# GpSimd's turn on the shared port is taken from the instruction in front of VectorE's last port user, with the port's release as traced and a new policy table

## The chip, the cores and the metric

The kernel runs on one core of one Trainium2 chip. The metric is the device time of one execution in microseconds (us). TensorE is called PE, VectorE DVE, ScalarE ACT, GpSimd POOL and SyncE SP, as in the profile; SP only issues DMAs here.

## The reference

```python
xn = layernorm(x)                                   # x: 1 x 2048 x 512, bf16
q, k, v = heads(xn @ wqkv)                          # 32 heads of 16
p = softmax(q @ k.T * 16 ** -0.5)                   # 2048 x 2048 in each head
A = (p @ v) @ wo
h = layernorm(xn)
u = gelu(einsum("bsd,sf->bdf", h, w1) + b1)         # along the sequence: 2048 -> 1376
B = transpose(einsum("bdf,fs->bds", u, w2) + b2)    # 1376 -> 2048
out = x + A + B
```

The attention takes nearly all of the time: 32 heads of 2048 x 2048 exponentials.

## The kernel before

**Tiles.** The scores are made in 1024 tiles of 128 x 1024: 32 blocks (a block is a quarter of the queries for four heads) times 16 groups of keys times two head pairs. PE writes a tile's scores into two PSUM banks (`L799`, two matmuls a tile; `L789` in the last block). The exponential of a tile is made in one of two ways. Either ACT makes it (name `exp`, `L825`), which gives one bf16 tile; or DVE makes it (name `dexp`, `L834`) by adding a constant and converting to int16, so that the bits read as bf16 are an approximate exponential. Such a tile then needs three more copies of itself with other constants added (`SHIFTS`, name `sh`, `L840`: int16 128 x 1024, SBUF to SBUF). The shifts are shared between DVE and POOL. PE multiplies each of the tiles with V (`L881`, `L870`, four matmuls a tile), so an ACT tile costs PE one such group and a DVE tile four. Where the two banks of a tile lie side by side, `exp` and `dexp` are one instruction of 1024 elements; otherwise they are two of 512.

**Other work.** Projections (`L929`, `L985`), the token mixing's two products (also `L929`), PSUM evictions on DVE (`L955`, `L974`, `L995`, `L1031`, `L1077`, `L1103`), small normalisation steps and the scaling of VM (`L635`, `L688`) and the division by the softmax sum (`L1142`) on POOL. `L726` are matmuls without use that keep PE's clock up where the plan leaves PE idle.

**Order.** A planner in the kernel's own Python (class `Sched` and the `while True` loop) decides, when the program is built, which engine does what and in which order. It has a cost for every operation, keeps the time at which each engine is free, and takes the candidate that can start first. The loop's choices are steered by a policy of eight numbers; `PLAN` is a string of 64 base-36 digits, one for each 16 tiles, that names the policy in `POLICIES`. The planned times are not in the program: it holds each engine's instructions in order, and semaphore waits between them.

**The shared port.** An operation with `port=True` is one that uses the SBUF port which DVE and POOL share: the shifts on both engines and all POOL work. The planner keeps `port_free` for both engines (when the port is free of that engine). `port_time` holds back the start of a port operation accordingly, `_time` sets `port_free`, and `add` makes each POOL operation wait, by a semaphore, for DVE's last port user:

```python
if port and eng == "pool" and self.port_op is not None:
    deps.add(self.port_op)
if port and eng == "dve":
    self.port_op = op
```

DVE never waits for POOL because of the port. In the loop, a POOL shift becomes a candidate only if the time until DVE's next port operation (or until DVE is free) is at least `SH_I` = 1.11 less a slack of the policy.

Of the kernel before, what the change touches and what calls it, by code (L numbers as in the profile page):

```python
# [58 lines left out]
SEM = 0.05  # L59
PE_SWITCH = 0.10  # L60
PE_LAT = 0.38
PV_T = 0.1095
POOL_AFTER = 0.03
AS_I, AS_L = 0.8, 0.9
EXP_I, EXP_L = 0.904, 1.03
EXPH_I, EXPH_L = 0.477, 0.60
# [17 lines left out]
SH_I, SH_L = 1.11, 1.05  # L84
# [12 lines left out]
PLAN_STEP = 16  # L97
PLAN = tuple(int(c, 36) for c in "00f41j96ioe4283j88076r8jjti283fos8rs08tig23g0ih10n7tg0i05608f5v6")
URGENT = ("kv0", "qt", "kt", "vt")
URG_DUE = 24  # L100
UT0, UT_STEP = 196, 31
# [8 lines left out]
class Op:  # L110
# [3 lines left out]
    def __init__(self, eng, fn, name=""):  # L114
        self.eng = eng
        self.fn = fn
        self.pos = -1
        self.deps = []
        self.signals = False
        self.waits = []  # L120
        self.is_dma = False
        self.dma_sem = None
        self.dma_val = 0
        self.q = None
        self.after = None
        self.name = name
        self.t0 = 0.0
        self.t1 = 0.0


class Sched:
    ENGS = ("pe", "act", "dve", "pool", "sp")

    def __init__(self, nc, es):
        self.nc = nc
        self.es = es
        self.streams = {e: [] for e in self.ENGS}
        self.order = []
        self.last_writer = {}
        self.readers = {}  # L140
        self.dma_ops = []
        self.free = {e: 0.0 if e in ("sp", "act") else 0.7 for e in self.ENGS}
        self.busy = {e: 0.0 for e in self.ENGS}
        self.pe_mode = None
        self.pe_end = 0.0
        self.pe_tiles = {}
        self.port_free = {"dve": 0.0, "pool": 0.0}
        self.port_op = None
        self.act_end = 0.0
        self.pe_work = []  # L150
        self.filler = None
        self.pend = []
# [85 lines left out]

    def port_time(self, eng, t):

        return max(t, self.port_free["pool"] if eng == "dve" else self.port_free["dve"] + POOL_AFTER)

    def _time(self, op, cost, ready, port):
        eng = op.eng
        if port:
            ready = self.port_time(eng, max(self.free[eng], ready))
        if op.is_dma:
            op.t0 = max(self.free[eng], ready)
            self.free[eng] = op.t0 + cost[0]
            op.t1 = op.t0 + cost[1]  # L250
        elif eng == "pe":
            mode, tiles, dur = cost
            t = max(self.free["pe"], ready)
            if mode != self.pe_mode:
                t = max(t, self.pe_end + PE_SWITCH)
                self.pe_mode = mode
                self.pe_tiles = {}
            for x in tiles:
                t = max(t, self.pe_tiles.get(x, 0.0))
            for x in tiles:  # L260
                self.pe_tiles[x] = t + dur
            self.pe_end = max(self.pe_end, t + dur)
            self.free["pe"] = t + 0.004
            self.busy["pe"] += dur * len(tiles) / 4.0
            op.t0, op.t1 = t, t + dur + PE_LAT - 0.214
            self.pe_work.append((t, dur, len(tiles) / 4.0))
        else:
            op.t0 = max(self.free[eng], ready)
            self.free[eng] = op.t0 + cost[0]
            self.busy[eng] += cost[0]  # L270
            op.t1 = op.t0 + cost[1]
            if eng == "act":
                op.t1 = max(op.t1, self.act_end + cost[0] + (EXP_GAP if op.name == "exp" else 0.0))
                self.act_end = op.t1
                self.free[eng] = max(self.free[eng], op.t1 - ACT_QUEUE)
        if port:
            self.port_free[eng] = op.t0 + cost[0]

    def add(self, eng, fn, reads=(), writes=(), name="", dma=False, out_dma=False, cost=None, port=None):
        op = Op(eng, fn, name)  # L280
        op.is_dma = dma
        op.q = "o" if out_dma else "i"
        if cost is None:
            cost = (DMA_I, DMA_L) if dma else (("F", (0, 1, 2, 3), 0.22) if eng == "pe" else (EV_I, EV_L))
        deps = self._deps(eng, reads, writes, dma)
        deps.discard(op)
        if port is None:
            port = eng == "pool" and not dma
        ready = self.ready(eng, reads, writes, dma)
        if eng == "pe" and self.filler is not None:  # L290
            self.pend = [k[1] for k in writes if k[0] == "bank"] if name == "sc" and cost[2] > 0.2 else []
            self.keep_clock(ready, cost)
        self._time(op, cost, ready, port)
        if port and eng == "pool" and self.port_op is not None:
            deps.add(self.port_op)
        if port and eng == "dve":
            self.port_op = op
        op.deps = list(deps)
        for k in reads:
            self.readers.setdefault(k, []).append(op)  # L300
        for k in writes:
            self.last_writer[k] = op
            self.readers[k] = []
        op.pos = len(self.streams[eng])
        self.streams[eng].append(op)
        self.order.append(op)
        if dma:
            self.dma_ops.append(op)
        return op
# [79 lines left out]
def bass_parallel_sum__softmax_full_mha__mixer_token_mlp__prompt_kernel(  # L389
# [18 lines left out]
    with ExitStack() as es:  # L408
# [415 lines left out]
        def exp_specs(n):  # L824
            return [dict(eng="act", fn=lambda e, cs=cs, src=src: e.activation(buf(pbuf[n])[:, cs], src, ACTF.Exp, scale=LN2_128),  # L825
                         reads=[("bank", k) for k in ks], writes=half_keys(free_p[0], cs), name="exp",
                         cost=(EXP_I, EXP_L) if side(n) else (EXPH_I, EXPH_L)) for cs, src, ks in parts(n)]
# [5 lines left out]
        def dexp_spec(n, w):  # L833
            return [dict(eng="dve", fn=lambda e, cs=cs, src=src: e.tensor_scalar(  # L834
                buf_i(w)[:, cs], src, IBIAS, 0.0, ALU.add, ALU.max),
                reads=[("bank", k) for k in ks], writes=half_keys(w, cs), name="dexp",
                cost=(P1_I, P1_L) if side(n) else (P1H_I, P1H_L)) for cs, src, ks in parts(n)]
# [491 lines left out]
        def h_ok():  # L1329
            return next_n >= H_AT + H_STEP * h_n[0] and all(("xT", t) in have for t in range(NT))  # L1330
# [45 lines left out]
        def est(specs):  # L1376
            s0 = specs[0]
            r = 0.0
            for s_ in specs:
                r = max(r, sc.ready(s_["eng"], s_["reads"], s_["writes"]))  # L1380
            t = max(sc.free[s0["eng"]], r)
            if s0.get("port"):
                t = sc.port_time(s0["eng"], t)
            return t
# [102 lines left out]
        while True:  # L1487
            if next_n >= plan_at and plan_at < NN:
                d_steal, p_keep, dead_slack, pe_fit, ext_rank, d_back, d_fly, p_slack = POLICIES[PLAN[plan_at // PLAN_STEP]]
                plan_at += PLAN_STEP  # L1490
# [11 lines left out]
            if ready_q and free_p:  # L1502
                el = []
                for n in ready_q:
                    sp_ = exp_specs(n)
# [6 lines left out]
            if ready_q and fly < d_fly and len(free_p) >= 4 + p_keep:  # L1512
                act_free = sc.free["act"]
                for qi, n in enumerate(ready_q):
                    if NN - n <= D_END:
                        continue
                    sp_ = dexp_spec(n, free_p[0])
                    t = est(sp_)
# [6 lines left out]
            for j in sh_jobs:  # L1525
                if j["ok"]():
                    sp_ = shift_spec("dve", j["w"], j["o"], j["k"])
# [11 lines left out]
            pl = []  # L1539
            dve_port = min([z[0] for z in dl if z[2] == "shd" or (z[2] == "gen" and z[3]["cur"][1][0].get("port"))] + [1e9])  # L1540
            for j in sh_jobs:
                if NN - j["n"] <= POOL_END:
                    continue
                sp_ = shift_spec("pool", j["w"], j["o"], j["k"])
                pl.append((est([sp_]), 1, "shp", (j, sp_), SH_I))
            for g in frees + exts:
                if g["cur"] and g["cur"][0] == "pool":
                    pl.append((est(g["cur"][1]), 0, "gen", g, 1.25))
            if hgen is not None and h_ok():
                pl.append((max(sc.free["pool"], next_h), 2, "h", None, 0.67))  # L1550
            pl = [z for z in pl if max(dve_port, sc.free["dve"]) - z[0] >= z[4] - p_slack]
# [6 lines left out]
            sp_, e_s = None, 1e9  # L1558
# [3 lines left out]
            if next_n < NN and pv_grp >= grp(vblk(next_n)) - 1 and len(free_banks) >= 2 + spare and score_has(next_n):  # L1562
                s_ = best_pair()
                banks_of[next_n] = s_
                sp_ = score_specs(next_n)
# [44 lines left out]
            if not cands:  # L1610
                pl = [z for z in ([] if not sh_jobs else [(0, 0, "shd", (sh_jobs[0], shift_spec("dve", sh_jobs[0]["w"], sh_jobs[0]["o"], sh_jobs[0]["k"])))])]
# [12 lines left out]
            elif kind == "exp":  # L1624
                n, sp_ = what
                ready_q.remove(n)
                exp_commit(n)
                for z in sp_:
                    add(z)
                free_banks.extend(banks_of[n])  # L1630
            elif kind == "dexp":
                n, sp_ = what
# [3 lines left out]
                for z in sp_:  # L1636
                    add(z)
# [8 lines left out]
            elif kind in ("shd", "shp"):  # L1646
                j, sp_ = what
# [15 lines left out]
            elif kind == "gen":  # L1663
                g = what
# [9 lines left out]
            elif kind == "score":  # L1674
                n, sp_, s_ = what
# [6 lines left out]
            elif kind == "pv":  # L1682
# [4 lines left out]
                if pv_left[b] == 0:  # L1687
                    g = dict(gen=task_spill() if b < 0 else task_epilogue(b) if b < NBLK - 1 else task_tail(b - NBLK + 1), cur=None)
# [4 lines left out]
            elif kind == "ext":  # L1693
                g = what
# [21 lines left out]
            for i, (rel, due, nm, gen, need) in enumerate(ext_tasks):  # L1716
# [19 lines left out]
                g = dict(gen=gen, cur=None, due=due, name=nm)  # L1736
# [63 lines left out]
```

## Time and profile before

| | |
|---|---|
| median of 3 runs | 698.47 us (698.19 to 698.93) |
| the profiled execution | 698.7 us |
| its span, first to last instruction | 696.8 us, 29995 instructions |
| PE busy | 686.3 us (98%), 13225 matmuls |
| ACT busy | 678.4 us (97%), 789 instructions |
| DVE busy | 663.6 us (95%), 1198 |
| POOL busy | 388.6 us (56%), 436 |
| granted PE clock | 1.000 |

The profiled execution lies 0.23 us above the median, and 1.9 us lie outside its span. Busy time is the union of an engine's instructions in the trace. Successive instructions of ACT and of DVE overlap in the records (the next one begins before the one in front has ended), so the cost of one in a row of them is taken from end to end, not from its recorded duration.

### The profile page before, as it was taken

How to read it: one execution, taken by the hardware profiler on the slowest of the kernel's cores; microseconds unless marked ns; L12 is line 12 of the kernel's file. 1: busy time of each engine (PE TensorE's matmuls, PEld its weight loads, DVE VectorE, ACT ScalarE, POOL GpSimd, SP SyncE). 2: the span in 40 equal slices, each digit the busy share in tenths (PEclk: the TensorE clock that was granted, in tenths of full speed). 3: DMA queues.
4: the chain of work that ended last, by engine and by line, in shares of the span. 5: the costliest groups of instructions: out<-in, count | busy, mean ns of one | idle time of the engine just before them, and what ended most of it. 6: DMA issues, size and time to landing. Idle time of an engine off the chain costs nothing.

```text
span 696.8 us, 29995 instructions
## 1 busy us (share of the span) xinstructions
PE 686.3 (98%) x13225; PEld 317.4 (46%) x13225; DVE 663.6 (95%) x1198; ACT 678.4 (97%) x789; POOL 388.6 (56%) x436
## 2 busy tenths in 40 slices
PE   8999999999999999999999999999999999999998
PEld 6544444444444444444454444444444444444444
DVE  7888979999999999998999999999999999989997
ACT  7999999999999999999999999999999999999996
POOL 6856744356565556555555565555555545545654
PEclk9999999999999999999999999999999999999999
DMA  7410131101122121220222213121220102112111
GB/s 225 66 25 13 45 79 27 30 6 32 43 45 56 40 61 41 49 56 20 43 48 59 63 31 79 45 49 29 47 61 23 48 25 64 46 45 63 38 30 45
DMA packets 88756, 33.86 MB, mean 49 GB/s; under 512 B 70514, under 2 KB 88626, under 8 KB 88626
## 3 DMA queue, kind: packets, MB, share of 16 engines
q1 hardware_dynamic: 87810, 31.56, 19.4%
q8 instruction: 103, 1.69, 1.0%
q10 hardware_dynamic: 816, 0.39, 0.2%
q14 instruction: 27, 0.22, 0.1%
HBM read 21.70 MB, written 2.35 MB: 35 GB/s over the span
## 4 chain that ended last, share of the span: by engine, by line
PE 65%; DVE 22%; ACT 9%; issue 2%; POOL 1%; DMA 1%; DVEq 0%; POOLq 0%
PE ps L881 23%; PE ps L799 23%; PE ps L929 16%; DVE pT L834 8%; ACT pT L825 7%; DVE pT L840 5%; DVE x_sb L834 3%; ACT x_sb L825 2%; DVE x_sb L840 2%; PE ps L985 1%; DVE OT L1103 1%; DMA xnT<-hx 1%; PE ps L870 0%; DVE Qall L955 0%; DVE osb L1077 0%
## 5 line engine op out<-in xcount | busy, mean ns | idle before, releaser
L825 ACT ACTIVATE pT<-ps 128x1024 bf16<-128x1024 f32 (+1 forms) x570 | 528.3, 1105 | 5.3 <-PE ps L799 5.2
L799 PE MATMUL ps<-QT,KT 32*128 32x512 bf16 x1976 | 276.0, 384 | 1.8 <-DVE pT L834 0.4
L834 DVE TENSOR_SCALAR pT<-ps 128x1024 int16<-128x1024 f32 (+1 forms) x265 | 263.6, 1011 | 10.1 <-PE ps L799 9.8
L881 PE MATMUL ps<-pT,V 128*32 128x256 bf16 x4624 | 245.0, 275 | 1.4 <-DVE OT L1103 0.3
L840 POOL TENSOR_SCALAR pT<-pT 128x1024 int16<-128x1024 int16 x158 | 165.1, 1045 | 124.0 <-DVE pT L840 86.5
L825 ACT ACTIVATE x_sb<-ps 128x1024 bf16<-128x1024 f32 (+1 forms) x197 | 201.2, 1089 | 1.2 <-PE ps L799 1.2
L799 PEld LDWEIGHTS ps<-QT,KT 32*128 32x128 bf16 x1976 | 76.7, 91 | 169.9 <-ACT pT L825 72.7
L881 PEld LDWEIGHTS ps<-pT,V 128*32 128x32 bf16 x4624 | 111.4, 96 | 73.8 <-issue 52.7
L840 DVE TENSOR_SCALAR pT<-pT 128x1024 int16<-128x1024 int16 x317 | 127.6, 428 | 0.4
L834 DVE TENSOR_SCALAR x_sb<-ps 128x1024 int16<-128x1024 f32 (+1 forms) x110 | 110.8, 1022 | 2.7 <-PE ps L799 1.8
L881 PE MATMUL ps<-x_sb,V 128*32 128x256 bf16 x1712 | 109.1, 275 | 0.4 <-DVE x_sb L840 0.3
L840 POOL TENSOR_SCALAR pT<-x_sb 128x1024 int16<-128x1024 int16 x64 | 66.9, 1045 | 49.9 <-DVE pT L840 39.0
L840 POOL TENSOR_SCALAR x_sb<-pT 128x1024 int16<-128x1024 int16 x57 | 59.6, 1045 | 38.3 <-DVE pT L840 27.5
L881 PE MATMUL ps<-pT,VM 128*32 128x256 bf16 x912 | 64.7, 275 | 0.9 <-POOL VM L688 0.5
L929 PE MATMUL ps<-hx,wblk 128*32 128x512 bf16 x688 | 59.9, 384 | 0.0
L881 PEld LDWEIGHTS ps<-x_sb,V 128*32 128x32 bf16 x1712 | 43.8, 96 | 25.4 <-issue 19.5
L840 DVE TENSOR_SCALAR pT<-x_sb 128x1024 int16<-128x1024 int16 x133 | 54.3, 429 | 0.2
L840 DVE TENSOR_SCALAR x_sb<-pT 128x1024 int16<-128x1024 int16 x110 | 45.9, 424 | 0.1
L929 PE MATMUL ps<-wkv_raw,wblk 128*32 128x512 bf16 x512 | 44.6, 385 | 0.0
L1142 POOL TENSOR_TENSOR oT<-oC,denb 128x256 bf16<-128x256 f32 (+1 forms) x32 | 23.3, 728 | 29.5 <-DVE pT L840 16.2
L840 POOL TENSOR_SCALAR x_sb<-x_sb 128x1024 int16<-128x1024 int16 x24 | 25.1, 1045 | 18.5 <-DVE pT L840 15.6
L881 PEld LDWEIGHTS ps<-pT,VM 128*32 128x32 bf16 x912 | 24.2, 96 | 15.7 <-issue 9.7
(124 smaller groups left out, 461.4 us busy)
## 6 DMA issues: line engine op xcount, KB each, us to landing
wblk<-in_B_w_dram SPq DMA_DIRECT2D x10, 512.0 KB, 4.6
wblk<-in_B_w_dram SPq DMA_DIRECT2D x16, 320.0 KB, 3.6
oC<-OT SPq DMA_DIRECT2D x248, 16.0 KB, 1.9
denb<-rden_scratch SPq DMA_DIRECT2D x124, 32.0 KB, 1.9
xr<-in_A_x_dram SPq DMA_DIRECT2D x16, 128.0 KB, 2.3
out_dram<-osb SPq DMA_DIRECT2D x16, 128.0 KB, 2.0
QT<-Qall SPq DMA_DIRECT2D x120, 16.0 KB, 1.9
x_sb<-in_A_x_dram SPq DMA_DIRECT2D x2, 512.0 KB
```

The source lines that it names most:

```text
L799: specs.append(dict(eng="pe", fn=lambda e, r=r, bk=bk: e.matmul(bank(bk), lhsT=KT[32 * r:32 * r + 32, T, 128 * kt:128 * (kt + 1)], rhs=QT[ ...
L825: return [dict(eng="act", fn=lambda e, cs=cs, src=src: e.activation(buf(pbuf[n])[:, cs], src, ACTF.Exp, scale=LN2_128), reads=[("bank", k) ...
L834: return [dict(eng="dve", fn=lambda e, cs=cs, src=src: e.tensor_scalar(buf_i(w)[:, cs], src, IBIAS, 0.0, ALU.add, ALU.max), reads=[("bank" ...
L840: return dict(eng=eng, fn=lambda e: e.tensor_scalar(buf_i(o), buf_i(w), float(SHIFTS[k]), 1.0, ALU.add, ALU.mult), reads=[("pT", w), ("pTh ...
L881: specs.append(dict(eng="pe", fn=lambda e, c=c, h=h, i=i, off=off: e.matmul(bank(pv_bank[vb])[32 * c:32 * c + 32, 256 * par:256 * par + 25 ...
L929: specs.append(dict(eng="pe", fn=lambda e, c=c, w=w: e.matmul(bank(ex)[32 * c:32 * c + w, :], lhsT=lhs_of(32 * c, 32 * c + w), rhs=rhs, st ...
L985: specs.append(dict(eng="pe", fn=lambda e, ct=ct, c=c, i=i, t=t: e.matmul(bank(ex)[32 * c:32 * c + 32, 128 * i:128 * (i + 1)], lhsT=xnT[:, ...
L1103: yield "pvev", [dict(eng="dve", name="pvev", fn=lambda e: e.tensor_copy(OT32[:, eb, :], bank(pv_bank[b])), reads=[("bank", pv_bank[b])], ...
L1142: yield "pool", [dict(eng="pool", fn=lambda e, cs=cs: e.tensor_tensor(oT[0:m, qb % NOT, T, cs], oC32[0:m, tb_, cs], denb[0:m, tb_, cs], AL ...
```

## The change

The wait of a POOL port operation is moved one DVE instruction forward: where the plan has DVE's last port user directly behind the instruction in front of it (less than 0.03 between them), POOL waits for that instruction in front, and otherwise for the port user itself, as before. The planner's times of the port follow: POOL may start 0.06 before DVE's port user is through (it was 0.03 after), and DVE may have the port at POOL's planned end less 0.14 (it was POOL's full issue time). The window that a POOL shift needs shrinks accordingly. The string `PLAN` is new; the policies are the same.

```diff
-POOL_AFTER = 0.03
+POOL_AFTER, PORT_EARLY, PORT_DVE = 0.03, 0.06, 0.14
...
-PLAN = tuple(int(c, 36) for c in "00f41j96ioe4283j88076r8jjti283fos8rs08tig23g0ih10n7tg0i05608f5v6")
+PLAN = tuple(int(c, 36) for c in "e0f71tkefn1205ne7vn8e80s81sod0fozj8fd8gs0arg8ihle0i285gw0r2e60te")
...
     def port_time(self, eng, t):
-        return max(t, self.port_free["pool"] if eng == "dve" else self.port_free["dve"] + POOL_AFTER)
+        if eng == "dve":
+            return max(t, self.port_free["pool"])
+        if self.port_dep is not None:
+            t = max(t, self.port_dep.t1 + SEM + POOL_AFTER)
+        return max(t, self.port_free["dve"] - PORT_EARLY)
...
         if port:
-            self.port_free[eng] = op.t0 + cost[0]
+            self.port_free[eng] = op.t0 + (cost[0] if eng == "dve" else cost[1] - PORT_DVE)
...
+        was_free = self.free[eng]
         self._time(op, cost, ready, port)
-        if port and eng == "pool" and self.port_op is not None:
-            deps.add(self.port_op)
+        if port and eng == "pool" and self.port_dep is not None:
+            deps.add(self.port_dep)
         if port and eng == "dve":
-            self.port_op = op
+            st = self.streams["dve"]
+            self.port_dep = st[-1] if st and op.t0 - was_free < 0.03 else op
...
-                pl.append((est([sp_]), 1, "shp", (j, sp_), SH_I))
+                pl.append((est([sp_]), 1, "shp", (j, sp_), SH_L - PORT_DVE))
...
-                    pl.append((est(g["cur"][1]), 0, "gen", g, 1.25))
+                    pl.append((est(g["cur"][1]), 0, "gen", g, 1.05))
```

(`SH_I, SH_L` = 1.11, 1.05, issue time and latency of a POOL shift.) Since the planner decides everything, the whole order changes. The two built programs hold, engine by engine:

| | before | after |
|---|---|---|
| exponentials on ACT, 1024 / 512 elements | 665 / 102 | 682 / 70 |
| tiles on ACT / on DVE | 716 / 304 | 717 / 303 |
| `dexp` on DVE, 1024 / 512 elements | 233 / 142 | 254 / 98 |
| shifts on DVE | 609 | 579 |
| shifts on POOL | 303 | 330 |
| matmuls of score tiles with V | 7744 | 7732 |
| runs of score matmuls on PE, other work between them | 689 | 677 |
| clock-keeping matmuls `L726` | 292 | 352 |
| DMAs issued by SP | 668 | 668 |

All other instructions are equal in number. Four tiles of the start are made in a way of their own, and are not in the second row. Lines behind the edit lie six lines lower in the kernel after (`L840` is `L846` there).

More of the change, by code (lines that the diff above doesn't have):

```diff
@@ L147, in __init__ @@
         self.port_free = {"dve": 0.0, "pool": 0.0}
-        self.port_op = None
+        self.port_dep = None
         self.act_end = 0.0
```

## The prediction

> **What bounds the kernel now.** I read the page's busy shares first, then the costliest groups.
>
> ```profile
> PE 686.3 (98%) x13225; PEld 317.4 (46%) x13225; DVE 663.6 (95%) x1198; ACT 678.4 (97%) x789; POOL 388.6 (56%) x436
> ...
> L825 ACT ACTIVATE pT<-ps 128x1024 bf16<-128x1024 f32 (+1 forms) x570 | 528.3, 1105 | 5.3 <-PE ps L799 5.2
> ...
> L840 POOL TENSOR_SCALAR pT<-pT 128x1024 int16<-128x1024 int16 x158 | 165.1, 1045 | 124.0 <-DVE pT L840 86.5
> ```
>
> Three engines are nearly full; POOL, whose waits the change shortens, is not. So I asked which of the three leaves time that something can give back. ACT's exponentials follow each other, end to end, every 0.917 us (1024 elements) or 0.490 us (512); I took each interval in the trace above that as a hole. After the first 50 us only 13 places lose much: one is the table load around the gelu, and 12 are holes of 0.47 to 0.66 us, 0.564 on average, 6.8 us together. The rest of the 50 to 690 us is exponentials back to back. A smaller loss of 0.47 us stands at 41 us. The last exponential ends at 690.0; the tail behind it takes 6.8 us. So the kernel's time is ACT's list of exponentials, plus holes, plus start and tail.
>
> The timeline around one hole, PE and ACT:
>
> ```profile
> 486.94 0.44 PE L799 MATMUL ps<-QT,KT 32*128 32x512 bf16 x4
> 487.31 0.40 PE L929 MATMUL ps<-gT_hi,wblk 128*32 128x512 bf16 x4
> ...
> 487.76 0.50 PE L881 MATMUL ps<-pT,V 128*32 128x256 bf16 x12
> 488.09 0.60 PE L929 MATMUL ps<-xnT,wq_sb 128*32 128x512 bf16 x8
> ...
> 488.75 0.47 PE L799 MATMUL ps<-QT,KT 32*128 32x512 bf16 x4
> ...
> 489.18 1.02 ACT L825 ACTIVATE pT<-ps 128x1024 bf16<-128x1024 f32 x1 [0.40 <-PE ps L799]
> ```
>
> PE made two tiles of scores at 486.94, then a long run of other matmuls, and the next scores only at 488.75. I set a PE cost on such runs: 0.11 us for four matmuls with V, 0.21 for four projection matmuls (the rows above, in which a further group of four adds that). All 12 holes, and nothing else after 50 us, have this form: a run of at least 0.95 us, in front of which the last scores were a pair of which DVE took one tile, so that ACT had one exponential (0.92 us) to last over it. Outside the gelu stage, none of the 22 equally long runs in front of which both tiles went to ACT made a hole.
>
> **The port.** Cycle of DVE and POOL, from the timelines of the two engines:
>
> ```profile
> 297.00 0.42 DVE L840 TENSOR_SCALAR pT<-x_sb 128x1024 int16<-128x1024 int16 x1
> 297.33 1.22 DVE L834 TENSOR_SCALAR x_sb<-ps 128x1024 int16<-128x1024 f32 x1
> 298.47 0.41 DVE L840 TENSOR_SCALAR pT<-x_sb 128x1024 int16<-128x1024 int16 x1
> ```
>
> ```profile
> 297.50 1.05 POOL L840 TENSOR_SCALAR pT<-x_sb 128x1024 int16<-128x1024 int16 x1 [0.76 <-DVE pT L840]
> ```
>
> POOL's shift starts 0.083 us behind the recorded end of DVE's last shift (297.42; median of all turns) and lasts 1.045. DVE's next shift ends here 0.34 behind POOL's end, which is no stall: DVE came straight from its 1.13 us `dexp`. Where DVE comes sooner, its shift is drawn out and ends 0.279 us behind POOL's end, to a few ns each time: 25 shifts, 7.5 us in all, for instance
>
> ```profile
> 330.82 0.82 DVE L840 TENSOR_SCALAR x_sb<-x_sb 128x1024 int16<-128x1024 int16 x1
> ```
>
> against a POOL shift from 330.31 to 331.36. The opposite case, which the change makes the rule, is in the trace too: POOL released while a DVE shift runs.
>
> ```profile
> 48.05 0.42 DVE L840 TENSOR_SCALAR pT<-pT 128x1024 int16<-128x1024 int16 x1
> 48.22 0.75 POOL L688 TENSOR_SCALAR VM<-V 128x544 bf16<-128x544 bf16 x1 [0.77 <-DVE V L995]
> ```
>
> This L688 lasts 0.746 instead of the usual 0.646: it was held 0.10 us, and worked as if started at 48.32, 0.146 us ahead of the recorded end of DVE's shift (48.47). L688 at 31.75 and L635 at 86.02 show the same; L635 at 94.28, with two shifts in a row ahead of it, was held 0.35 us. So POOL loses the port to a DVE shift that began 0.17 us earlier, and then starts 0.083 + 0.146 = 0.23 us earlier than a turn of today.
>
> **The change part by part.**
>
> *The wait.* In the program after, 289 of POOL's 330 shifts wait for the instruction in front of DVE's last shift, 41 for that shift itself. From the end of DVE's last shift, the next DVE shift can end after 0.083 + 1.045 + 0.279 = 1.41 us today, after -0.146 + 1.045 + 0.279 = 1.18 us then. Behind a waiting POOL shift only POOL work is queued, and PE with the matmuls of that tile, which has three other tiles to go on with. I price the wait itself at nothing on the path; DVE's next shift is its cover.
>
> *DVE's load.* 30 shifts less by 0.335 (end to end in a row): -10.05 us. `dexp`: (254 - 233) x 1.133 - (142 - 98) x 0.598 = -2.5. New stalls at the port: for each turn I set its POOL work against the DVE work that the order puts between two shifts. That gives 18.5 us for the order before, of which the trace shows 7.5; and 23.2 us for the order after, so 9.4 by the same share, 23.2 at most: +1.9, at most +15.7. DVE's sum: -10.7, at worst +3.1, against 33.2 us that it idles now (696.8 - 663.6). None of it is on the path, since no hole of ACT was DVE's.
>
> *POOL.* 27 shifts more: 28 us on 388.6 busy of 696.8. Free.
>
> *PE.* 12 matmuls with V less (3 x 0.11 us), 12 alternations between scores and other work less; the 60 more clock-keeping matmuls lie where PE waits. At most some 3 us less on PE, which counts only as holes of ACT; these are next. SP's DMAs are as many as before.
>
> *ACT's list.* 17 x 0.917 - 32 x 0.490 = -0.09 us.
>
> *ACT's holes.* In the order after I count runs of the kind that made all 12 holes: 9 (1.42, 1.22, 1.22, 1.19, 1.40, 1.30, 1.18, 0.98 and 1.19 us). 3 x 0.564 = -1.7. Two of the 9 come behind a run that left ACT two tiles more, and two further runs are near the bound: 7 to 11, which is -2.8 to -0.6. The run in front of the loss at 41 us shrinks from 1.03 to 0.92: -0.1. The gelu stage has other runs in the new order (1.74, 3.26 and 1.93 us for 3.32 and 2.52), which I take at nothing, 0.5 either way.
>
> *Tail.* Behind the last scores stand 64 matmuls with V, for 52: 3 x 0.11 = +0.3, bounds 0 and 0.7.
>
> Sum: -0.1 - 1.7 - 0.1 + 0.3 = -1.6 us. The profiled 698.7 becomes 697.1; the median lies 0.2 lower: **696.9 us**.
>
> **The rivals.**
>
> *A, the forecast:* -1.6, by the bounds above -3.5 to +0.4, 695.0 to 698.9.
>
> *B, more holes close.* The relieved DVE frees PSUM banks sooner and PE alternates less, so that half of the remaining nine close too: 4.5 x 0.564 = 2.5, 694.4. For it: in the list of waits, PE's weight loads for scores waited 28.3 us for L834. Against: none of the 12 holes ended on DVE.
>
> *C, slower: the long runs behind two ACT tiles begin to starve ACT.* The order before has 22 runs of 0.95 us and more behind such a pair, the order after 36. None cost anything before, up to 1.56 us long (after: up to 1.50). But a run of 1.4 us with the scores behind it takes up nearly the two exponentials (1.83 us); a plan that packs tighter leaves less behind. From six new holes it is slower by more than 0.2%; at nine, 9 x 0.564 - 1.6 = +3.5, 702.0.
>
> *D, slower: POOL gets the port ahead of DVE's last shift,* where that shift is not started by then. The shift would end 0.083 + 1.045 + 0.279 = 1.41 behind the one in front instead of 0.335: 1.07 us each. DVE's slack (33.2 + 10.7) carries 41 such turns of 289; 60 would cost 20 us, 717. Against it: DVE's shifts start 0.08 ahead of the end of the one in front, and together they idled under 1 us before; POOL lost each time in the trace. The Trainium skill ("SBUF — State Buffer", Who interferes with whom) says that whoever issues first gets the shared pair for the whole instruction. The rows at 48 us agree: DVE was 0.17 us ahead, and kept it.
>
> *E, the change doesn't do what it says: the turn starts no earlier.* Then the new order's narrow windows stall DVE by 36.8 us on my count instead of 23.2, by the traced share 14.9: DVE +7.4 - 12.5, still under its idle time; half a hole or two more, about 697.8. The Trainium skill ("SBUF — State Buffer", A bandwidth-pool intuition that's wrong) gives this rule: GpSimd is blocked until DVE's end and about 115 ns more; by it the turn would start 0.03 us later than today's 0.083, not earlier. The trace differs: 0.146 us ahead of the end, on the rows at 48 us.
>
> **How the numbers follow.** Within 0.2% (1.4 us) the measurement can hardly tell from no change: 697.1 to 699.9. A 0.50 (faster 0.28, same 0.20, slower 0.02), B 0.20 (faster), C 0.15 (slower), D 0.06 (slower), E 0.09 (faster 0.03, same 0.05, slower 0.01). That makes faster 0.51, same 0.25, slower 0.24. The range 693.5 to 701.0 holds A, E, most of B and the nearer half of C. A's own range is 695.0 to 698.9.
>
> **What would show it.** Right: POOL shifts that begin within DVE's last shift and last some 1.15 us, with ends 0.9 behind that shift's end; DVE shifts drawn out to 0.28 behind POOL's end, 10 to 20 us in all; DVE busy some 10 us less; 7 to 11 ACT holes after 50 us, each at the runs named. Wrong: holes behind two ACT tiles (C), DVE shifts of 1.4 us behind POOL (D), POOL starts 0.08 behind DVE's end (E), or ACT waits that end on DVE.

## The result

| | median of the runs | ratio to before on the same chip, 95% interval |
|---|---|---|
| before | 698.82 us (20 runs) | |
| after | 699.57 us (20 runs) | 1.0015 [1.0008, 1.0021] |

The changed kernel is slower by 0.75 us, by the interval 0.6 to 1.5; 696.9 was forecast. 699.57 lies in the wide range of the prediction (693.5 to 701.0) and above that of its case A (695.0 to 698.9). The profiled execution has a span of 697.6 us, before it was 696.8.

The page of the changed kernel, busy shares and the costliest groups that answer to those shown of before (lines have moved by six: the exponential is now `L831`, `dexp` `L840`, the shifts `L846`, scores `L805`):

```profile
PE 685.1 (98%) x13273; PEld 317.9 (46%) x13273; DVE 665.0 (95%) x1145; ACT 679.1 (97%) x774; POOL 441.1 (63%) x463
...
L831 ACT ACTIVATE pT<-ps 128x1024 bf16<-128x1024 f32 (+1 forms) x544 | 510.7, 1089 | 4.4 <-PE ps L805 4.0
...
L846 POOL TENSOR_SCALAR pT<-pT 128x1024 int16<-128x1024 int16 x174 | 192.3, 1105 | 108.0 <-DVE pT L846 63.7
L846 DVE TENSOR_SCALAR pT<-pT 128x1024 int16<-128x1024 int16 x305 | 128.9, 448 | 0.9
```

DVE has 53 instructions fewer and is busy 1.4 us longer (665.0 for 663.6); it was to be some 10 us less. Its shifts into `pT` from `pT` last 448 ns on average, for 428 before, and POOL's 1105 where they lasted 1045.

The timeline of DVE and POOL around one turn:

```profile
237.60 0.42 DVE L846 TENSOR_SCALAR x_sb<-pT 128x1024 int16<-128x1024 int16 x1
237.94 0.42 DVE L846 TENSOR_SCALAR pT<-pT 128x1024 int16<-128x1024 int16 x1
238.11 1.15 POOL L846 TENSOR_SCALAR pT<-pT 128x1024 int16<-128x1024 int16 x1 [0.98 <-DVE x_sb L846]
238.28 0.69 DVE L961 TENSOR_SCALAR Qall<-ps 128x512 bf16<-128x512 f32 x1
238.89 0.65 DVE L846 TENSOR_SCALAR pT<-pT 128x1024 int16<-128x1024 int16 x1
```

This is the cycle that the change wanted. POOL is released by the shift of 237.60, begins at 238.11, 0.25 us ahead of the end of DVE's last shift (238.36), and lasts 1.15 instead of 1.045: it was held for 0.11 us. It ends at 239.26. DVE came back too soon: its shift of 238.89 is drawn out to 0.65 and ends at 239.54, 0.28 behind POOL. I call what a DVE shift lasts beyond 0.418 us its **stall**; the trace has 61 stalled shifts with 21.7 us, before it had 25 with 7.5.

**An account of the time.** I split each trace at the end of the 21st exponential of 1024 elements (at 44.2 to 45.3 us in all the runs below; what lies ahead is start-up, which differs by up to 1.2 us between executions) and at the end of the last one. Between them lies the *stretch*: ACT's list, and its holes, split here into those above 0.1 us (without the two at the gelu, 0.92 to 0.93 us together) and the sum of all lesser ones. Behind it lies the tail. The last column is DVE's share of the page's chain: the work that ended last, followed back from the last instruction, at each step to what released it. The runs come from several chips; the median of before on them is 698.70 to 698.82 us.

| run | median us | stalls us (count) | DVE idle, 100 to 650 us | holes over 0.1, us | lesser, us | stretch, us | tail, us | DVE in the chain |
|---|---|---|---|---|---|---|---|---|
| before | 698.82 | 7.5 (25) | 12.3 | 6.97 | 0.60 | 645.21 | 6.80 | 22% |
| after | 699.57 | 21.7 (61) | 13.9 | 7.52 | 0.91 | 646.00 | 7.24 | 25% |
| e1 old order, early turn | 698.27 | 4.4 (20) | 13.2 | 6.69 | 0.63 | 644.97 | 6.74 | 19% |
| e4 old order, short POOL shifts | 698.41 | 0.6 (3) | 14.7 | 6.66 | 0.63 | 644.93 | 6.79 | 18% |
| e8 old order, delayed turn | 710.65 | 23.3 (166) | 11.0 | 15.42 | 3.23 | 656.29 | 7.49 | 64% |
| e2 new order, late turn | 708.15 | 28.9 (64) | 13.6 | 14.53 | 2.04 | 654.13 | 7.47 | 43% |
| e3 new order, short POOL shifts | 698.18 | 3.3 (18) | 22.5 | 6.42 | 0.18 | 644.16 | 7.22 | 5% |
| e9 new order, 54 short | 698.24 | 4.6 (22) | 21.8 | 6.37 | 0.37 | 644.31 | 7.23 | 9% |
| e10 new order, the other 276 short | 698.75 | 15.1 (39) | 17.0 | 7.73 | 0.25 | 645.54 | 7.23 | 12% |
| e11 after, once more | 699.74 | 21.2 (59) | 13.9 | 7.39 | 1.01 | 645.97 | 7.23 | 24% |

After against before: the stretch is 0.79 us longer (holes over 0.1 us +0.55, lesser ones +0.31, the list 682 x 0.917 + 70 x 0.490 for 665 x 0.917 + 102 x 0.490 = -0.09), the tail 0.44; start-up was 0.51 shorter in this execution. That is chance: in e11, the same kernel, it was 0.11 longer than before's.

The nine large holes stand at the nine runs that the prediction named (0.58, 0.68, 0.72, 0.45, 0.91, 0.52, 0.39, 0.59 and 0.76 us, 5.59 together; before, 12 with 6.77). Beside them are nine small ones of 0.10 to 0.39 us, 1.94 together, eight at runs of PE of 0.44 to 0.87 us and one at 1.40 us; before, only one of 0.21 was in that class.

### The profile page after: what moved, and what is told of

The parts are those of the page before. It is cut to its first block, busy times and chain, and to the rows that moved or that the text cites. A ratio compares the mean times of both kernels' runs of the same rounds, so it can differ in the third digit from the quotient of the medians.

```text
span 697.6 us, 30069 instructions
## 1 busy us (share of the span) xinstructions
PE 685.1 (98%) x13273; PEld 317.9 (46%) x13273; DVE 665.0 (95%) x1145; ACT 679.1 (97%) x774; POOL 441.1 (63%) x463
## 4 chain that ended last, share of the span: by engine, by line
PE 59%; DVE 25%; ACT 13%; issue 2%; POOL 1%; POOLq 0%; DVEq 0%
PE ps L887 21%; PE ps L805 20%; PE ps L935 15%; DVE pT L840 11%; ACT pT L831 9%; DVE pT L846 6%; DVE x_sb L840 3%; DVE x_sb L846 3%; ACT x_sb L831 3%; PE ps L991 1%; DVE OT L1109 1%; POOL pT L846 1%; PE ps L709 1%; ACT pT L1432 0%; DVE V L1001 0%
## 5 line engine op out<-in xcount | busy, mean ns | idle before, releaser
L831 ACT ACTIVATE pT<-ps 128x1024 bf16<-128x1024 f32 (+1 forms) x544 | 510.7, 1089 | 4.4 <-PE ps L805 4.0
L805 PE MATMUL ps<-QT,KT 32*128 32x512 bf16 x1976 | 272.8, 384 | 4.5 <-DVE pT L840 2.0
L840 DVE TENSOR_SCALAR pT<-ps 128x1024 int16<-128x1024 f32 (+1 forms) x254 | 265.4, 1057 | 6.6 <-PE ps L805 6.2
L846 POOL TENSOR_SCALAR pT<-pT 128x1024 int16<-128x1024 int16 x174 | 192.3, 1105 | 108.0 <-DVE pT L846 63.7
L831 ACT ACTIVATE x_sb<-ps 128x1024 bf16<-128x1024 f32 (+1 forms) x208 | 214.9, 1093 | 1.6 <-PE ps L805 1.5
L805 PEld LDWEIGHTS ps<-QT,KT 32*128 32x128 bf16 x1976 | 75.9, 91 | 173.5 <-ACT pT L831 65.5
L846 DVE TENSOR_SCALAR pT<-pT 128x1024 int16<-128x1024 int16 x305 | 128.9, 448 | 0.9
L840 DVE TENSOR_SCALAR x_sb<-ps 128x1024 int16<-128x1024 f32 (+1 forms) x98 | 106.7, 1099 | 3.2 <-PE ps L805 3.2
L846 POOL TENSOR_SCALAR pT<-x_sb 128x1024 int16<-128x1024 int16 x71 | 77.9, 1098 | 35.8 <-DVE pT L846 20.7
L846 POOL TENSOR_SCALAR x_sb<-pT 128x1024 int16<-128x1024 int16 x61 | 68.0, 1115 | 33.3 <-DVE pT L846 19.6
L887 PE MATMUL ps<-pT,VM 128*32 128x256 bf16 x872 | 61.7, 274 | 0.5 <-POOL pT L846 0.3
L935 PE MATMUL ps<-hx,wblk 128*32 128x512 bf16 x688 | 57.3, 384 | 0.0
L846 DVE TENSOR_SCALAR pT<-x_sb 128x1024 int16<-128x1024 int16 x132 | 56.2, 448 | 0.3
L846 DVE TENSOR_SCALAR x_sb<-pT 128x1024 int16<-128x1024 int16 x108 | 50.3, 476 | 0.3
L1148 POOL TENSOR_TENSOR oT<-oC,denb 128x256 bf16<-128x256 f32 (+1 forms) x32 | 25.4, 793 | 21.6 <-DVE pT L846 14.5
L846 POOL TENSOR_SCALAR x_sb<-x_sb 128x1024 int16<-128x1024 int16 x24 | 27.3, 1140 | 14.9 <-DVE pT L846 11.4
L887 PEld LDWEIGHTS ps<-pT,VM 128*32 128x32 bf16 x872 | 23.2, 96 | 10.7 <-issue 6.1
```

Source lines behind the costliest of these rows:

```text
L805: specs.append(dict(eng="pe", fn=lambda e, r=r, bk=bk: e.matmul(bank(bk), lhsT=KT[32 * r:32 * r + 32, T, 128 * kt:128 * (kt + 1)], rhs=QT[ ...
L846: return dict(eng=eng, fn=lambda e: e.tensor_scalar(buf_i(o), buf_i(w), float(SHIFTS[k]), 1.0, ALU.add, ALU.mult), reads=[("pT", w), ("pTh ...
L887: specs.append(dict(eng="pe", fn=lambda e, c=c, h=h, i=i, off=off: e.matmul(bank(pv_bank[vb])[32 * c:32 * c + 32, 256 * par:256 * par + 25 ...
L935: specs.append(dict(eng="pe", fn=lambda e, c=c, w=w: e.matmul(bank(ex)[32 * c:32 * c + w, :], lhsT=lhs_of(32 * c, 32 * c + w), rhs=rhs, st ...
L1148: yield "pool", [dict(eng="pool", fn=lambda e, cs=cs: e.tensor_tensor(oT[0:m, qb % NOT, T, cs], oC32[0:m, tb_, cs], denb[0:m, tb_, cs], AL ...
```

## The experiments

The theories at the outset, which the expectations call 1, 2 and 3. **Stalls** (1): the early turn works, but the new order's narrow windows draw out DVE's shifts, and DVE hands that on to PE and ACT. **Order** (2): the new order itself has worse runs of PE. **Turn** (3): starting POOL inside DVE's shift costs something by itself. A fourth, the reserve of the old order, stands with e8.

### e1: the early turn alone, in the order of before

```diff
+        was_free = self.free[eng]
...
-            self.port_op = op
+            st = self.streams["dve"]
+            self.port_op = st[-1] if st and op.t0 - was_free < 0.03 else op
```

> The kernel before, order of every engine unchanged, table and planner's times unchanged; only POOL's waits are moved to the instruction in front of DVE's last port user, where the plan has the two back to back. Theory 1 (port stalls: what took the gain away is that the new order stalls DVE at the port for 21.7 us instead of 7.5): the turn alone cuts the stalls of this order from 7.5 to some 3 to 5 us; since no hole of ACT in this order ended on DVE, the time stays: -0.4 to +0.2 us against before. Theory 2 (the new order itself, not the port): the same. Theory 3 (the early wait itself costs, because a POOL instruction held at the port slows DVE): slower than before by 0.6 us or more, with the same order.

Measured: 698.27 us, before on the same chip 698.76; ratio 0.9998 [0.9989, 1.0008], no difference that can be told. The turn did move: 222 of POOL's 303 shifts now begin inside DVE's last one, and none did before. Stalls fell from 7.5 to 4.4 us, and the same 12 holes stayed. In an order that has room for POOL, the turn itself neither costs nor buys anything beyond the uncertainty of some 0.7 us.

### e2: the order of after, with the turn taken from the last port user

```diff
-            deps.add(self.port_dep)
+            deps.add(self.port_last)
...
+            self.port_last = op
```

> The kernel after, order of every engine unchanged; POOL waits again for DVE's last port user itself, as in the kernel before. Theory 1: DVE's shifts are stalled 30 to 37 us instead of 21.7, and the time is 1.5 to 4 us above after. Theory 2: stalls rise likewise, but the time stays within 0.4 us of after. Theory 3: faster than after by 0.5 us or more.

Measured: 708.15 us, ratio 1.0135 [1.0121, 1.0149], 8.6 us above the changed kernel, where theory 1 expected 1.5 to 4. So the early turn does what it is for: without it the new order is slower by that much. Its page, the busy shares and the first line of the chain that ended last:

```profile
PE 686.3 (97%) x13273; PEld 315.2 (45%) x13273; DVE 673.3 (95%) x1145; ACT 683.5 (97%) x774; POOL 417.2 (59%) x463
...
PE 44%; DVE 43%; ACT 6%; POOL 3%; issue 3%; DVEq 0%; POOLq 0%
```

The stalls rose by 7.2 us (21.7 to 28.9; 30 to 37 were expected) and the stretch by 8.1: here as much reaches the end as was added. DVE idles about as long (13.6 us from 100 to 650, after 13.9), so its idle time took up none of it.

### e3 and e4: both orders with POOL shifts of half as many elements

`buf_i32` is the tile's 2048 bytes a partition seen as 512 int32 in place of 1024 int16. The instruction reads and writes the same bytes with half the elements; what changes is the arithmetic, since the constant is then added to pairs of values as one number, so that the copies are not the shifted ones. Where an expectation below speaks of half the tile being left out, that is inexact in this sense: all of the tile is still read and written.

```diff
+            bi = buf_i32 if eng == "pool" else buf_i
...
-                buf_i(o), buf_i(w), float(SHIFTS[k]), 1.0, ALU.add, ALU.mult),
+                bi(o), bi(w), float(SHIFTS[k]), 1.0, ALU.add, ALU.mult),
```

> The kernel after, order unchanged; POOL's shifts work on 512 int32 elements instead of 1024 int16, which leaves out the exact shift (the numbers are not those of the reference) and takes roughly half POOL's time, so that DVE is hardly stalled. Theory 1: blocked DVE shifts fall from 21.7 us to under 5, the nine small holes of ACT go, the nine large ones stay; 1.5 to 2.7 us below after, that is 0.8 to 2 us below before. Theory 2: the blocked shifts fall but the small holes stay; within 0.4 us of after.

> The kernel before, order unchanged; POOL's shifts work on 512 int32 elements instead of 1024 int16, as in the run beside it. Theory 1: blocked DVE shifts fall from 7.5 us to under 2, the 12 holes stay; 0 to 0.5 us below before, so that of the two orders without stalls the new one is faster by 1 us or more. Theory 2: the same for this run, but then the old order stays ahead of the new one by 0.4 us or more.

Measured: e3 698.18 us, 0.999 [0.9982, 0.9999]; e4 698.41, 0.9995 [0.9986, 1.0004]. A POOL shift, with what it is held, lasts 0.73 us in e3 and 0.62 in e4 (medians), and the stalls are almost gone. With them gone the new order is 0.23 us ahead by the medians, 0.77 in the stretch and 0.43 behind in the tail. Its nine large holes take 5.08 us and e4's twelve 6.66; that 5.08 is 9 x 0.564 to the hundredth is luck, since single ones run from 0.39 to 0.90. But seven small holes of 1.34 us together stay in e3, and e4 has none: they come with the order for the most part (e3 still has 3.3 us of stalls). So the order gives little, and the stalls take more than that.

Neither theory had its numbers. Theory 1 wanted e3 1.5 to 2.7 us below the changed kernel, the small holes gone, and the new order ahead of the old by 1 us or more; e3 is 1.4 below by the medians, and keeps seven of the nine. Theory 2 wanted e3 within 0.4 us of the changed kernel and the old order ahead by 0.4.

### e9, e10 and e11: are the stalls the price, or POOL's later results?

Short POOL shifts also finish their tiles earlier. e9 shortens only the 54 shifts that stalled DVE in the trace of after; e10 shortens all others.

```diff
+                    shift_n.append(0)
+                    if len(shift_n) - 1 in BLOCKERS:        # e10: not in
+                        bi = buf_i32
```

> The changed kernel with its order as it stands; of GpSimd's shifts, the 54 that draw out a VectorE shift in its trace (18.9 of the 21.7 us of stalls) work on 512 int32 columns, half the tile, and the other 276 stay whole. Left out: the second half of those 54 tiles. Theory (the stalls at the port are what the new order gives back): 1.0 to 1.6 us less than the changed kernel on the same chip, blocked time under 6 us. Rival (what helped when all shifts were halved was that GpSimd's tiles were ready earlier, not that VectorE was let go): within 0.4 us of the changed kernel.

> The complement: the 54 GpSimd shifts that draw out a VectorE shift stay whole, the other 276 work on 512 int32 columns. Left out: the second half of those 276 tiles. Theory of the stalls: within 0.4 us of the changed kernel, blocked time still 18 to 20 us. Rival (earlier tiles): 1.0 us or more less than the changed kernel.

> The changed kernel once more, beside the two others on the same chip: 0.5 to 1.0 us more than the kernel before, by both theories.

Measured: e9 698.24 us, 0.9997 [0.9988, 1.0006]; e10 698.75, 1.0001 [0.9992, 1.001]; e11 699.74, 1.0014 [1.0005, 1.0024], 1.04 us above before. e9 is 1.5 us below the changed kernel with 54 of 330 shifts touched, as the theory of the stalls had it, and its stretch is that of e3 but for 0.15 us. The rival's "within 0.4" is refuted.

e10 is a miss for the theory: 1.0 us below e11 where 0.4 was the bound, as good as the 1.0 that the rival asked; it has 15.1 us of stalls where 18 to 20 were expected. In the traces it is only 0.43 us ahead in the stretch: shorter shifts elsewhere left DVE 3.1 us more idle time, the lesser holes fell from 1.01 to 0.25 us, and those over 0.1 us rose by 0.34. But one hole of 0.61 us in that trace has no counterpart in e9 or e11, which have the same order. There PE stood still in the middle of a row of its matmuls, for nothing that the profile shows (timeline of e10):

```profile
108.47 0.57 PE L1007 MATMUL ps<-wkv_raw,xnT 128*32 128x128 bf16 x28 [0.59 <-issue]
...
110.50 1.02 ACT L840 ACTIVATE pT<-ps 128x1024 bf16<-128x1024 f32 x1 [0.50 <-PE ps L805]
```

Without that hole the stretch would be 1.04 us ahead, as the medians say. What gives this is not separated. Its stalls fell by 6.1 us; at the rate of e9 (16.6 us of stalls for 1.66 us of stretch) I estimate 0.6 us for that. The rest, 0.4 us, can be POOL's earlier tiles. POOL itself has 1 to 2% of the chain in all of after, e9, e10 and e11, while DVE falls from 24% in e11 to 12% in e10 and 9% in e9. So the stalls are the larger part, the 54 shifts being worth more by the traces than the other 276, and a share of earlier tiles is not excluded; it can be in e9's gain too.

What a stall does is best seen at one place. Timeline of DVE, POOL, scores and ACT in the changed kernel:

```profile
184.31 0.59 DVE L846 TENSOR_SCALAR pT<-x_sb 128x1024 int16<-128x1024 int16 x1
184.70 0.79 POOL L1148 TENSOR_TENSOR oT<-oC,denb 128x256 bf16<-128x256 f32 x1
184.82 0.95 DVE L846 TENSOR_SCALAR x_sb<-x_sb 128x1024 int16<-128x1024 int16 x1
185.69 1.21 DVE L840 TENSOR_SCALAR pT<-ps 128x1024 int16<-128x1024 f32 x1
186.96 0.40 PE L805 MATMUL ps<-QT,KT 32*128 32x512 bf16 x4 [0.55 <-DVE pT L840]
187.43 1.97 ACT L831 ACTIVATE x_sb<-ps 128x1024 bf16<-128x1024 f32 x2 [0.26 <-PE ps L805]
```

and the same place in e9:

```profile
184.10 0.95 DVE L861 TENSOR_SCALAR pT<-x_sb 128x1024 int16<-128x1024 int16 x1
184.97 0.41 DVE L861 TENSOR_SCALAR x_sb<-x_sb 128x1024 int16<-128x1024 int16 x1
185.31 1.21 DVE L849 TENSOR_SCALAR pT<-ps 128x1024 int16<-128x1024 f32 x1
186.57 0.10 PEld L805 LDWEIGHTS ps<-QT,KT 32*128 32x128 bf16 x4 [0.65 <-DVE pT L849]
186.57 0.40 PE L805 MATMUL ps<-QT,KT 32*128 32x512 bf16 x4 [0.37 <-DVE pT L849]
187.04 1.02 ACT L840 ACTIVATE x_sb<-ps 128x1024 bf16<-128x1024 f32 x1
```

After has two drawn-out shifts (0.59 and 0.95), e9 one. PE's scores wait for `dexp` to give back the banks, 0.55 us in after and 0.37 in e9, and ACT's hole is 0.363 us in after and 0.188 in e9: the 0.18 us passes from DVE through PE to ACT. In the page's chain DVE has the smaller share in e9, after first:

```profile
PE 59%; DVE 25%; ACT 13%; issue 2%; POOL 1%; POOLq 0%; DVEq 0%
```

```profile
PE 61%; ACT 27%; DVE 9%; POOL 2%; issue 1%; POOLq 0%; DVEq 0%
```

### e8: stalls put into the old order

A tiny memset on POOL ahead of each of its shifts delays the shift, with no other change of the order. POOL's shifts then begin 0.216 us behind the end of DVE's last one (median), for 0.083 before.

```diff
-            return dict(eng=eng, fn=lambda e: e.tensor_scalar(
+            return dict(eng=eng, fn=lambda e: (e.memset(dly[:, n_dly(): n_dly.i], 0.0) if eng == "pool" else None, e.tensor_scalar(
```

> The kernel before, order unchanged but for one small memset (16 x 1) that POOL does in front of each of its shifts, with the wait of that shift: the turn at the port starts some 0.17 us later (0.09 for the memset, 0.08 to the next start). Theory 4 (reserve: the old planner held DVE off until 1.475 us behind the start of DVE's last shift, the trace has 1.406, so its order has 0.07 us of reserve in each turn; the new planner uses the traced value and leaves none): a delay beyond the reserve stalls DVE by about 0.11 us in the some 145 turns that have one dexp as cover, 16 us in all, and the time rises by 8 to 16 us. Rival (the old order is insensitive because its holes are not DVE's, as its run with early turns seemed to say): stalls rise, the time by 1.5 us at most.

Measured: 710.65 us, 1.0169 [1.0155, 1.0183]. The stalls rose by 15.8 us (166 drawn-out shifts), the stretch by 11.1, all of it holes of ACT (over 0.1 us +8.45, lesser +2.63). The page's chain by engine:

```profile
DVE 64%; PE 24%; ACT 7%; issue 3%; POOL 1%; DVEq 0%; POOLq 0%
```

DVE leads it here, with 22% in before. The rise, 11.9 us on the same chip, lies in the 8 to 16 expected, and the rival's 1.5 is refuted. So the old order, too, hands stalls on to the end; that none of its holes was DVE's did not make it safe. That its reserve in each turn is 0.07 us was worked out from the planner's numbers and not tested apart.

### e7: the tail

The output matmuls wait for POOL's last divisions, `L1148`. In the changed kernel (timeline):

```profile
689.70 1.63 POOL L1148 TENSOR_TENSOR oT<-oC,denb 64x256 bf16<-64x256 f32 x2 [2.30 <-DVE pT L846]
691.38 0.40 PE L935 MATMUL ps<-wo_c,oT 128*32 128x512 bf16 x4 [0.17 <-POOL oT L1148]
```

e7 frees that last pair, named `oT_end` there, from waiting for the port.

```diff
-        if port and eng == "pool" and self.port_dep is not None:
+        if port and eng == "pool" and self.port_dep is not None and name != "oT_end":
```

> The kernel after, order unchanged; only the last division of POOL (the two L1148 of the block before the last, 64 rows) no longer waits for DVE's turn at the port, but for its data alone. In the profile after, these two start at 689.70 behind DVE's last shifts, and the output matmuls that need them stand 0.45 us later than before. If the longer tail (7.24 us behind ACT's last exponential, 6.79 before) comes from that wait, the tail falls to 6.8 or 6.9 and the time by 0.3 to 0.5 us against after. If it comes from the 12 matmuls with V more behind the last scores (the prediction's term), the tail stays at 7.2 within 0.1.

Measured: 700.42 us, 1.0026 [1.0015, 1.0036]; the tail grew from 7.24 to 7.58 us. In e7's timeline the divisions take the port early and two DVE instructions are drawn out by it:

```profile
687.79 1.87 POOL L1148 TENSOR_TENSOR oT<-oC,denb 64x256 bf16<-64x256 f32 x2
688.13 0.95 DVE L1200 TENSOR_TENSOR OT<-denb,rcomp 128x256 bf16<-128x256 f32 x1
689.00 0.95 DVE L846 TENSOR_SCALAR x_sb<-x_sb 128x1024 int16<-128x1024 int16 x1
```

The expectation fell: the wait was cheaper than the collision. What makes the new tail 0.44 us longer was not settled.

### e5 and e6: the new code with the old table, the old code with the new table

```diff
e5, against after:  PLAN = the string of before
e6, against before: PLAN = the string of after
```

> The change's planner with the old table, one part of the change alone; the order is another one again: 720 tiles on ACT and 300 on DVE (716 and 304 before), 14 runs of the kind that makes holes. ACT's list alone is 3.7 us longer. If the planner's times without their table were the gain, this would be faster than before; I expect 4 to 8 us slower than before, since table and planner's times go together.

> The old planner with the new table, the other part alone: 723 tiles on ACT and 297 on DVE, 14 runs of the kind that makes holes. ACT's list alone is 6.4 us longer; I expect 6 to 11 us slower than before. If the table alone were what moved the time, this would be within 1 us of after.

Measured: e5 707.21 us, 1.0128 [1.0109, 1.0148]; e6 710.86, 1.0176 [1.0162, 1.0189]. They are 8.4 and 12.1 us slower than before, each just above what was expected (4 to 8, 6 to 11). Neither half of the change stands alone, but for a reason that has little to do with the port: with the wrong table ACT's list is longer, 661 x 0.917 + 118 x 0.490 = 664.0 us in e5 and 647 x 0.917 + 152 x 0.490 = 667.8 in e6, for 659.8 before, and its holes over 0.1 us grow by 2.8 and 3.2. Stalls are 16.6 and 6.8 us. So these two tell next to nothing of the port.

## Why the prediction was wrong

The forecast was -1.6, the medians say +0.75. Its terms, set against what the runs allow to take apart (e3 less e4 for the order almost without stalls; the stretch of after less that of e3, less the same for before and e4, for the stalls, so that whatever POOL's earlier tiles give in e3 and e4 is in that row too):

| term | forecast, us | measured, us |
|---|---|---|
| ACT's list | -0.09 | -0.09 |
| large holes, 12 to 9 | -1.7 | -1.58 |
| small holes over 0.1 us of the order | none | +1.34 |
| lesser holes of the order | none | -0.45 |
| port stalls | none | 1.84 - 0.28 = +1.56 |
| tail | +0.3 | +0.44 |
| loss at 41 us | -0.1 | -0.03 |
| sum | -1.6 | +1.2 |

The sum of the measured column is the two traces without the chance of start-up; the medians, with more executions, put it at 0.75, and 1.2 lies in their interval.

*Port stalls* are the step that failed, under "DVE's load", in three places. First, the scaling: the count from the order gave 18.5 us for before, of which the trace showed 7.5, and I carried that share over, 23.2 to 9.4. The count itself was nearly right for the new order: 21.7 measured. For the late turn it gave 36.8, I scaled it to 14.9, and e2 has 28.9. The share measured in the old order did not hold in the new one. Second, the room: I set the stalls against 33.2 us of idle DVE time, but only 12.3 of these lie between 100 and 650 us. The windows of the traces, 100 to 650 us, the columns PE, PEld, DVE, ACT and POOL busy; first before, then after, then e9:

```profile
100.00:650.00 550.00, 546.79 (x10452) 244.81 (x10451) 537.73 (x942) 545.44 (x621) 301.94 (x303) 1.00 0.20 45
```

```profile
100.00:650.00 550.00, 544.86 (x10481) 244.97 (x10481) 536.14 (x884) 544.34 (x608) 347.11 (x326) 1.00 0.20 46
```

```profile
100.00:650.00 550.00, 545.91 (x10506) 246.28 (x10504) 528.17 (x886) 545.28 (x609) 329.27 (x326) 1.00 0.20 46
```

DVE does have less to do in the new order (528.17 with the blockers short), and the stalls fill that relief up again, to 536.14. The worst case of the step, +3.1 us for DVE, held the 1.4 measured, but it was priced at nothing. Third, "none of it is on the path, since no hole of ACT was DVE's" read too much from the holes of before: at 186.96 PE's scores wait for a late `dexp`, and ACT's hole behind it stands in PE's name. So none of the rivals A to E is what happened; of the prediction's own signs, DVE busy some 10 us less failed, and the 10 to 20 us of drawn-out shifts came as 21.7.

*The holes.* The nine large ones came at the runs named. What the count missed was its bound of 0.95 us, which held for the old order alone: the new one has small holes at runs of 0.44 to 0.87 us, five of the nine behind a pair of which DVE took one tile.

*The port, as forecast:* 212 of POOL's 330 shifts begin inside DVE's last one and last 1.153 us (median); they end 0.90 behind its end, and a stalled shift ends 0.28 behind POOL's end.

*Rival C:* the price was wrong and the mechanism nearly absent; of the 36 long runs behind two ACT tiles none makes a hole over 0.17 us in after (the one of 0.61 in e10 is PE's stray halt). *Rival D* did not occur. *Rival E* is refuted by the starts; its price, 697.8, was 10 us too low (e2, 708.15), for the same scaling. *Rival B* is refuted too: in e9 DVE is relieved (21.8 us idle) and all nine large holes stay, 5.07 us together.

No version here that keeps the arithmetic beats before by more than can be told: e1, e3 and e9 lie 0.5 to 0.6 us below it, e1 and e9 within the uncertainty, e3 (0.999 [0.9982, 0.9999]) barely outside it, and e3 and e9 change the shifts' arithmetic.

## What to carry to other kernels

Idle time of an engine is room only in the stage where the load comes: cut start and tail off before you set a new cost against it. A count of stalls from the order was an upper bound in all three cases here (18.5 for 7.5, 23.2 for 21.7, 36.8 for 28.9): price the bound, not a share of it carried over from another order, and follow it to who waits for the stalled engine. The price per stall is not constant: e9's 17 us less of stalls were worth 1.7 us of the stretch, but e2's 7 us more cost 8. A planner that hands a resource over earlier gained nothing here, where its table spent the gain on a tighter fit.

## What the runs showed of the port

A waiting POOL shift loses to the DVE shift in progress but resumes 0.144 us before that shift's recorded end (start 0.253 ahead of it, held 0.109; medians of 212 turns). The Trainium skill ("SBUF — State Buffer", A bandwidth-pool intuition that's wrong) speaks of a lock, and gives "blocked until DVE-end + ~115 ns" beside a DMA whose descriptors GpSimd can't write until DVE releases the port. The waiting shows in the held POOL shifts here, but they resume ahead of DVE's end; a DMA of that kind is another case, which no run here has. What I had not expected is how steep the price becomes: in e2 the turn comes 0.23 us later (0.083 behind the end of DVE's shift, as in before, instead of 0.144 ahead of it), and that costs 8.6 us.
